# Token gather of the first feed-forward group moved behind the experts' matrix products, conversions given later steps, and the last output stored in four pieces

## The chip, the cores and the metric

The kernel runs on one core of one Trainium2 chip. The metric is the device time of one execution in microseconds (us). A core has five instruction streams, each in order: TensorE (PE in the rows; its weight loads are PEld), VectorE (DVE), ScalarE (ACT), GpSimd (POOL) and SyncE (SP), which issues most of the DMA transfers. A name with a q behind it (SPq, ACTq) is the sequencer of that stream, which decodes, branches and waits.

## The reference, cut to what matters

Three layers follow each other on 3072 tokens of width 384. Attention by a delta rule over 768 positions gives x; a router picks one of eight experts for each token; then a dense feed-forward layer runs over all tokens. The change lies where the second and the third layer meet, and at the end of the third.

```python
for e in range(E):                      # experts, E = 8, F = 1024
    mask = e_idx == e
    h = np.maximum(x[mask] @ w1[e], 0.0)
    out[mask] = gate_w[mask, None] * (h @ w2[e])
...
h = x @ w_in                            # feed-forward, d_ff = 2048
g = h * (1.0 / (1.0 + np.exp(-h)))
return (g @ w_out).astype(np.float32)
```

Every product is made in three passes over operands split into a high and a low part (high times high, high times low, low times high), so one tile of 128 inner rows costs three matmuls.

## The kernel before

**Experts.** `Experts.regular` (L1111) walks nine slots of tokens, five of 256 and four of 512, and each slot in eight chunks of 128 hidden units: 72 steps. A step splits the chunk's two weight tiles (`split`, L1016 on ACT, L1017 on DVE; the tiles are called wRH for w1 and wKT for w2), makes the hidden units (`first`, nine matmuls of 128x512 into ph, L1057, then L1060 on ACT and L1061 on DVE) and adds the chunk before it into the output banks (`second`, twelve matmuls of 128x384 into poe, L1068). When a slot is done, four copies (L1093, ACT) put its rows into the buffers ysb, and four indirect DMAs of POOL (L1095) scatter them to the tokens' places in the DRAM tensor ys. The first chunk of the last slot is followed by a branch for tokens that exceed the nine slots (`extra`, L1159); it is not taken here.

**Feed-forward.** `Ffn` walks six groups of 512 tokens. `tokens(g)` (L1275) gathers a group: SP loads 768 KB of ys into fy (L1278), PE transposes it by 3 times 4 matmuls with the identity into the banks fpt (L1282), and ACT (L1283) and DVE (L1284) split it into fxh and fxl. `group` (L1287) then makes sixteen chunks f: `first(f)` is nine matmuls of 128x512 into fph (L1298), a sigmoid (L1301, ACT), a product (L1303, DVE) and the split into fgh (L1305, ACT) and fgl (L1307, DVE); `second(f)` is twelve matmuls of 128x384 into four output banks fpo (L1315), one for each block of 128 tokens. At the end four copies, two on ACT and two on DVE (L1334), and one store of SP (L1335) bring the group out. The group at index g reads the block (g + 3) % 6 of ys, so the first group reads block 3. The last slot of the experts writes blocks 0 to 2 only, so the first group has to wait for the last slot but one.

**What sets the order.** Instructions are traced in program order and then placed by a scheduler, which moves them inside each engine as their inputs allow. Three numbers of `PLAN` (L35) bear on the change. `tok` is the step behind which the gather of the first group is traced (L1450); `n0` and `npre` spread 40 pieces of weight conversion for the feed-forward layer over the steps (L1446): behind step i, (i + 1 - n0) * npre / (72 - n0) pieces have been traced. These conversions are loads of SP (L1176) and elementwise work of DVE and ACT (L1187 to L1196). `tc.issue_after(x)` is a rule for the scheduler: what is traced inside its block comes behind x on x's engine. `experts.mark` is the last traced matmul of L1068.

Of the kernel before, what the change touches and what calls it, by code (L numbers as in the profile page):

```python
# [31 lines left out]
    hold=[17, 19, 21, 13],  # L32


    fin=10, fin1=19, fin2=30, fin3=36, n0=37, npre=40, tok=68,  # L35
)


# [1161 lines left out]
class Ffn:  # L1200
# [86 lines left out]
    def group(self, g, x, nxt, fill=()):  # L1287
        nc, P = self.nc, self.P
        xh, xl = x
        po = [P[p].tile([128, 384], F32, tag=p, name=f"fpo{g}_{c}") for c, p in enumerate(("pm", "pm", "pa", "pa"))]  # L1290

        def first(f):
            fs = slice(128 * f, 128 * f + 128)
            ph = P["pa"].tile([128, 512], F32, tag="pa", name=f"fph{g}_{f}")
            n = 0
            for k in range(3):
                for a, b in ((self.ih, xh), (self.ih, xl), (self.il, xh)):
                    nc.tensor.matmul(ph, a[:, k, fs], b[:, k, :], start=(n == 0), stop=(n == 8))  # L1298
                    n += 1
            sg = self.take("sg")  # L1300
            nc.scalar.activation(sg, ph, AF.Sigmoid)  # L1301
            gv = self.take("gv")
            nc.vector.tensor_tensor(gv, ph, sg, op=ALU.mult)  # L1303
            gh = self.take("gh")
            self.marks = [nc.scalar.copy(gh, gv).ins]  # L1305
            gl = self.take("gl")
            self.marks.append(nc.vector.tensor_tensor(gl, gv, gh, op=ALU.subtract).ins)  # L1307
            return gh, gl

        def second(f, gh, gl):  # L1310
            oh, ol = self.o[f]
            for c in range(4):
                cs = slice(128 * c, 128 * c + 128)
                for i, (a, b) in enumerate(((gh, oh), (gh, ol), (gl, oh))):
                    nc.tensor.matmul(  # L1315
                        po[c], a[:, cs], b, start=(f == 0 and i == 0), stop=(f == 15 and i == 2)
                    )

        prev = None
        for f in range(16):  # L1320
            cur = first(f)
            for fn in fill[f : f + 1]:
                with self.tc.issue_after(self.marks[0]), self.tc.issue_after(self.marks[1]):
                    fn()
            if f == 8 and nxt is not None:
                self.x = self.tokens(nxt)
            if prev is not None:
                second(f - 1, *prev)
            prev = cur
        second(15, *prev)  # L1330
        yield
        ob = P["fo"].tile([128, 4, 384], F32, tag="ob", name=f"ob{g}")
        for c in range(4):
            (nc.vector.tensor_copy if c % 2 else nc.scalar.copy)(ob[:, c, :], po[c])  # L1334
        nc.sync.dma_start(self.out.rearrange("(b t p) d -> t p b d", b=4, p=128)[g], ob)  # L1335

    def run(self, x, fill, spare):

# [8 lines left out]
def cut(t, sizes):  # L1347

    out, at = [], 0
    for n in sizes:  # L1350
        out.append(t[:, at : at + n])
        at += n
    return out
# [6 lines left out]
def expert_buffers(ar, ld, fw, f):  # L1360

    b = {}
    b["raw1"] = [rest(ar.tile([128, 3072], F32, tag="KQ0", name="raw1"), 1024)]
    kb = ar.tile([128, 4096], F32, tag="KB", name="raw2")
    b["raw2"], b["ysb"] = [rest(kb[:, 0:3072], 384)], cut(kb[:, 3072:3840], [384] * 2)
    hs = cut(ar.tile([128, 1024], F32R, tag="KQ1", name="hs"), [256] * 4)
    b["hh"], b["hl"] = hs[0:2], hs[2:4]
    ws = sum((cut(ar.tile([128, 1536], F32R, tag=t, name=f"w{t}"), [384] * 4) for t in ("RH", "KT")), [])
    for i, name in enumerate(("h1", "l1", "h2", "l2")):
        b[name] = [rest(x, 128) if i < 2 else x for x in ws[2 * i : 2 * i + 2]]  # L1370
    xs = [rest(ld.tile([128, 768], F32R, tag="kr", name=f"xhl{i}", bufs=4), 256) for i in range(4)]
    b["xh"], b["xl"] = xs[0:2], xs[2:4]

    o = fw.tile([128, 6144], F32R, tag="o1", name="pairs")
    b["xh2"] = [f.bufs["xh"][0], rest(o[:, 0:1536], 512)]
    b["xl2"] = [f.bufs["xl"][0], rest(o[:, 1536:3072], 512)]
    hs = cut(o[:, 3072:5120], [512] * 4)
    b["hh2"], b["hl2"] = hs[0:2], hs[2:4]
    b["xg"] = cut(ld.tile([128, 768], F32, tag="sq", name="xg", bufs=1), [384] * 2)
    b["xg2"] = b["xg"] + cut(f.P["f0"].tile([128, 768], F32, name="xg2"), [384] * 2)  # L1380
    return b


def ffn_buffers(ar):

    b = {x: [rest(ar.tile([128, 1536], F32R, tag=t, name=f"f{x}2"), 512)] for x, t in (("xh", "RH"), ("xl", "KT"))}
    kb = cut(ar.tile([128, 4096], F32, tag="KB", name="fy2"), [1536] + [512] * 4)
    b["y"], b["sg"], b["gv"] = [rest(kb[0], 384)], kb[1:3], kb[3:5]
    b["gh"] = cut(ar.tile([128, 1024], F32R, tag="KQ1", name="fgh"), [512] * 2)
    b["gl"] = cut(ar.tile([128, 1024], F32R, tag="KQ0", name="fgl"), [512] * 2)  # L1390
    return b


@with_exitstack
def fused_kernel(ctx: ExitStack, tc, q, k, v, beta, mod, w_gate, bias, w1, w2, w_in, w_out, out):
    nc = tc.nc

    def pool(stack, name, bufs=1, **kw):
        return stack.enter_context(tc.tile_pool(name=name, bufs=bufs, **kw))

    N, D = out.shape
    P = {
        "dram": pool(ctx, "dram", space=DRAM), "cc": pool(ctx, "cc"),
        "pa": pool(ctx, "pa", 5, space=PSUM), "pm": pool(ctx, "pm", 3, space=PSUM),
    }
    ident = P["cc"].tile([128, 128], F32, name="ident")
    make_identity(nc, ident)

    xs = P["dram"].tile([N, D], F32, name="xs")
    ys = P["dram"].tile([N, D], F32, name="ys")  # L1410
    P["rc"] = pool(ctx, "rc")

    with ExitStack() as moe:
        for name in ("ar", "ld"):
            P[name] = pool(moe, name, side="right")
        rank = ExitStack()
        P["rs"] = pool(rank, "rs", side="right")
        with ExitStack() as att:
            for name in ("ac", "ln"):
                P[name] = pool(att, name)  # L1420
            for name in ("sm", "y"):
                P[name] = pool(att, name, 2)
            attn = Attention(tc, ident, P, q, k, v, beta, xs)
            router = Router(tc, ident, P, attn.B, attn.T, w_gate, bias, mod)
            attn.run(router.load, router.logits, router.gate, router.wave)
        P["fw"], P["f0"] = pool(ctx, "fw"), pool(ctx, "f0")
        f = Ffn(tc, ident, P, w_in, w_out, ys, out)
        experts = Experts(tc, ident, P, router, w1, w2, xs, ys, expert_buffers(P["ar"], P["ld"], P["fw"], f))
        raw = ctx.enter_context(ExitStack())
        P["fr"] = pool(raw, "fr", 2)  # L1430
        n0, n1, at = PLAN["n0"], 9 * 8, 0
        fill = []
        P["rb"] = Views([P["fw"].tile([128, 6144], F32, tag=tag, name="scratch") for tag in ("il", "o0")])
        for i, _ in enumerate(experts.regular()):
            if i == PLAN["fin"]:
                steps = router.wave(attn.T - 1)
                next(steps)
            if i in (PLAN["fin1"], PLAN["fin2"], PLAN["fin3"]):
                with tc.issue_after(experts.mark):
                    next(steps, None)  # L1440
            if i == PLAN["fin3"]:
                rank.close()
                room = pool(raw, "fe").tile([128, 1536], F32, name="ysb2")
                experts.bufs["ysb2"] = cut(room, [384] * 4)
                fill = f.chain(f.inner() + f.outer(range(0, 8), "o0"))
            to = max(0, (i + 1 - n0) * PLAN["npre"] // (n1 - n0))  # L1446
            for fn in fill[at:to]:
                fn()
            at = max(at, to)
            if i == PLAN["tok"]:  # L1450
                x0 = f.tokens(0)
        fill += f.chain(f.outer(range(8, 16), "o1"))

        def spare():
            raw.close()
            return pool(ctx, "fo", 2)

        f.add(ffn_buffers(P["ar"]))
        f.run(x0, fill[at:], spare)
# [32 lines left out]
```

## Time and profile before

| What | us |
|---|---|
| Median of 3 runs | 1022.76 |
| Lowest and highest run | 1019.37, 1027.38 |
| The profiled execution, its own time | 1020.31 |
| The profiled execution, its span | 1018.6 |
| PE busy in the span | 912.6 |

The span goes from the first to the last instruction of the profiled execution; 1.7 us of its own time lie around it. All rows below are from that execution, and their times are counted from the span's start. The attention fills the span to about 370 us, the experts' steps run to about 608 us, and the six feed-forward groups end at 1018.6 us. A releaser that a row names is inferred from semaphore events, and ends of matmuls are modelled.

### The profile page before, as it was taken

To read this page: it belongs to the slowest core of one execution; us is meant where nothing else is said; L and a number is where in the kernel's file an instruction comes from. 1 tells how busy PE (TensorE), PEld (TensorE's weight loads), DVE (VectorE), ACT (ScalarE), POOL (GpSimd) and SP (SyncE) were. 2 spreads that over 40 slices of the span, in tenths; PEclk is the share of its full clock that TensorE was granted. 3 is DMA by queue.
4 is the path that set the end of the run, shared out by engine and by line. 5 is a ranking of instruction groups with operands and counts; after the bars stand their busy time and mean duration, and the time that the engine had idled before them with its cause. 6 is when DMAs were issued, how large, how long until landed. Compare 5 with 4: busy or idle time off the path is not lost. (4 is left out here: it accounts for less than half of the span.)

```text
span 1018.6 us, 22789 instructions
## 1 busy us (share of the span) xinstructions
PE 912.6 (90%) x8934; PEld 823.1 (81%) x8934; DVE 653.8 (64%) x1802; ACT 531.3 (52%) x1142; POOL 140.7 (14%) x129
## 2 busy tenths in 40 slices
PE   4427788888889999999999799999999999999997
PEld 4426777777778988888889699999998989999996
DVE  7999998989984459999994246643334333333332
ACT  6655978888756746655664354433233323332322
POOL 5462311010200011242330101000000000000000
PEclk9776999999989999999999899999999999999999
DMA  6864444341454152176664121101001000000000
GB/s 131 169 141 87 89 110 95 88 105 43 106 167 92 50 174 90 40 236 218 221 203 136 63 82 61 62 32 32 1 32 32 7 25 1 32 1 1 32 1 31
DMA packets 157668, 84.42 MB, mean 83 GB/s; under 512 B 125449, under 2 KB 150039, under 8 KB 157552
## 3 DMA queue, kind: packets, MB, share of 16 engines
q1 hardware_dynamic: 154224, 73.04, 27.2%
q0 software_dynamic: 3328, 9.83, 3.0%
q8 instruction: 72, 1.18, 0.5%
q14 instruction: 44, 0.36, 0.1%
HBM read 69.74 MB, written 20.84 MB: 89 GB/s over the span
## 5 line engine op out<-in xcount | busy, mean ns | idle before, releaser
L1315 PE MATMUL fpo<-o,fgh 128*128 128x384 f32 x768 | 184.3, 338 | 0.0
L1303 DVE TENSOR_TENSOR fy<-fph,fy 128x512 f32<-128x512 f32 x96 | 66.4, 692 | 160.6 <-ACT fy L1301 160.1
L1315 PEld LDWEIGHTS fpo<-o,fgh 128*128 128x128 f32 x768 | 139.2, 188 | 7.9 <-ACT fgh L1305 0.4
L1301 ACT ACTIVATE fy<-fph 128x512 f32<-128x512 f32 x96 | 57.4, 598 | 168.1 <-PE fph L1298 165.1
L1315 PE MATMUL fpo<-o,fgl 128*128 128x384 f32 x384 | 116.6, 338 | 0.0
L1307 DVE TENSOR_TENSOR fgl<-fy,fgh 128x512 fp32r<-128x512 f32 x96 | 66.4, 692 | 76.0 <-ACT fgh L1305 65.7
L1298 PE MATMUL fph<-fxh,ih 128*128 128x512 f32 x288 | 113.7, 395 | 0.0
L1298 PE MATMUL fph<-fxl,ih 128*128 128x512 f32 x288 | 113.3, 394 | 0.0
L1298 PE MATMUL fph<-fxh,il 128*128 128x512 f32 x288 | 113.1, 393 | 0.0
L1305 ACT CAST fgh<-fy 128x512 fp32r<-128x512 f32 x96 | 59.7, 622 | 82.7 <-DVE fy L1303 44.3
L316 DVE TENSOR_TENSOR A<-A,tmp 128x126 f32<-128x126 f32 (+20 forms) x336 | 85.0, 288 | 0.2
L230 PE MATMUL gr<-RHs,KTs 128*128 128x128 f32 x384 | 60.1, 305 | 27.3 <-ACT KTs L219 14.7
L230 PEld LDWEIGHTS gr<-RHs,KTs 128*128 128x128 f32 x384 | 52.4, 212 | 35.9 <-ACT KTs L219 20.3
L1068 PE MATMUL poe<-wKT,pairs 128*128 128x384 f32 x384 | 77.2, 347 | 3.1 <-ACTq L1159 3.1
L308 DVE TENSOR_TENSOR tmp<-A,L 128x126 f32<-128x126 f32 (+20 forms) x336 | 77.3, 267 | 0.3
L1068 PEld LDWEIGHTS poe<-wKT,pairs 128*128 128x128 f32 x384 | 69.3, 193 | 6.6 <-ACTq L1159 3.5
L1315 PEld LDWEIGHTS fpo<-o,fgl 128*128 128x128 f32 x384 | 71.1, 188 | 0.5
L1016 ACT CAST wRH<-raw 128x384 fp32r<-128x384 f32 x72 | 36.8, 514 | 49.8 <-PE ph L1057 44.2
L1298 PEld LDWEIGHTS fph<-fxl,ih 128*128 128x128 f32 x288 | 54.1, 188 | 10.5
L1298 PEld LDWEIGHTS fph<-fxh,il 128*128 128x128 f32 x288 | 54.1, 188 | 9.6
L1298 PEld LDWEIGHTS fph<-fxh,ih 128*128 128x128 f32 x288 | 54.1, 188 | 9.0
L1017 DVE TENSOR_TENSOR wKT<-raw,wKT 128x384 fp32r<-128x384 f32 x72 | 39.9, 554 | 31.2 <-ACT wKT L1016 30.9
(427 smaller groups left out, 1838.0 us busy)
## 6 DMA issues: line engine op xcount, KB each, us to landing
raw<-in_moe_w_dram SPq DMA_DIRECT2D x72, 384.0 KB
kn<-KQ SPq DMA_DIRECT2D x12, 512.0 KB
ri<-in_moe_w_in_dram SPq DMA_DIRECT2D x12, 512.0 KB
ro<-in_moe_w_out_dram SPq DMA_DIRECT2D x16, 384.0 KB
kr<-in_k_dram SPq DMA_DIRECT2D x48, 96.0 KB
KQ<-in_q_dram SPq DMA_DIRECT2D x48, 96.0 KB
KI<-kn SPq DMA_DIRECT2D x48, 96.0 KB
Z<-in_v_dram SPq DMA_DIRECT2D x24, 192.0 KB
```

The costliest lines, as they stand in the source:

```text
L230: nc.tensor.matmul(gr[:, j], self.KT[r][:, k, w, :], RH[:, k, :, w, :], start=True, stop=True)
L308: nc.vector.tensor_tensor(tv, r[:, :, j : j + 1].to_broadcast([128, c, n]), L[:, j : j + 1, j + 1 :].to_broadcast([128, c, n]), op=ALU.mult,)
L316: ins = nc.vector.tensor_tensor(r[:, :, j + 1 :], r[:, :, j + 1 :], tv, op=ALU.add)
L1016: nc.scalar.copy(hi, raw)
L1017: nc.vector.tensor_tensor(lo, raw, hi, op=ALU.subtract)
L1068: self.mark = nc.tensor.matmul(po[t], a[:, cs], b, start=(c == 0 and i == 0), stop=(c == F - 1 and i == 2)).ins
L1298: nc.tensor.matmul(ph, a[:, k, fs], b[:, k, :], start=(n == 0), stop=(n == 8))
L1301: nc.scalar.activation(sg, ph, AF.Sigmoid)
L1303: nc.vector.tensor_tensor(gv, ph, sg, op=ALU.mult)
L1305: self.marks = [nc.scalar.copy(gh, gv).ins]
L1307: self.marks.append(nc.vector.tensor_tensor(gl, gv, gh, op=ALU.subtract).ins)
L1315: nc.tensor.matmul(po[c], a[:, cs], b, start=(f == 0 and i == 0), stop=(f == 15 and i == 2))
```

## The change

Four things are edited. `tok` goes from 68 to 70, and the gather of the first group is traced inside `issue_after(experts.mark)`. `n0` goes from 37 to 40, so the 40 pieces of conversion are spread over 32 steps in place of 35. In the last group, the matmuls of `second(14)` and `second(15)` are traced block by block, both chunks for one block of tokens before the next block. And the last group's output is stored by four DMAs of 192 KB, each traced behind the copy of its block, in place of one of 768 KB. The other groups keep their order.

```diff
--- before.py
+++ after.py
@@ -32,7 +32,7 @@
     hold=[17, 19, 21, 13],
 
 
-    fin=10, fin1=19, fin2=30, fin3=36, n0=37, npre=40, tok=68,
+    fin=10, fin1=19, fin2=30, fin3=36, n0=40, npre=40, tok=70,
 )
 
 
@@ -1307,13 +1307,13 @@
             self.marks.append(nc.vector.tensor_tensor(gl, gv, gh, op=ALU.subtract).ins)
             return gh, gl
 
-        def second(f, gh, gl):
+        def second(f, gh, gl, cs=range(4)):
             oh, ol = self.o[f]
-            for c in range(4):
-                cs = slice(128 * c, 128 * c + 128)
+            for c in cs:
+                rows = slice(128 * c, 128 * c + 128)
                 for i, (a, b) in enumerate(((gh, oh), (gh, ol), (gl, oh))):
                     nc.tensor.matmul(
-                        po[c], a[:, cs], b, start=(f == 0 and i == 0), stop=(f == 15 and i == 2)
+                        po[c], a[:, rows], b, start=(f == 0 and i == 0), stop=(f == 15 and i == 2)
                     )
 
         prev = None
@@ -1324,15 +1324,25 @@
                     fn()
             if f == 8 and nxt is not None:
                 self.x = self.tokens(nxt)
-            if prev is not None:
+            if prev is not None and (f < 15 or nxt is not None):
                 second(f - 1, *prev)
-            prev = cur
-        second(15, *prev)
+            if f < 15 or nxt is not None:
+                prev = cur
+        if nxt is not None:
+            second(15, *prev)
+        else:
+            for c in range(4):
+                second(14, *prev, range(c, c + 1))
+                second(15, *cur, range(c, c + 1))
         yield
         ob = P["fo"].tile([128, 4, 384], F32, tag="ob", name=f"ob{g}")
+        ov = self.out.rearrange("(b t p) d -> t p b d", b=4, p=128)[g]
         for c in range(4):
             (nc.vector.tensor_copy if c % 2 else nc.scalar.copy)(ob[:, c, :], po[c])
-        nc.sync.dma_start(self.out.rearrange("(b t p) d -> t p b d", b=4, p=128)[g], ob)
+            if nxt is None:
+                nc.sync.dma_start(ov[:, c], ob[:, c, :])
+        if nxt is not None:
+            nc.sync.dma_start(ov, ob)
 
     def run(self, x, fill, spare):
 
@@ -1448,7 +1458,8 @@
                 fn()
             at = max(at, to)
             if i == PLAN["tok"]:
-                x0 = f.tokens(0)
+                with tc.issue_after(experts.mark):
+                    x0 = f.tokens(0)
         fill += f.chain(f.outer(range(8, 16), "o1"))
 
         def spare():
```

What the built programs show of it, at three places. On PE, at the last slot of the experts, these rows stand around the gather before (poe1_12 to poe1_15 are the output banks of the slot's four token blocks, ph1_12_3 to ph1_12_7 its hidden chunks 3 to 7, fpt0_0 the first transposed part of the first group):

```order
L1057 MATMUL ph1_12_4_12604<-pairs_5842,wRH_5836 128x512 x2
L1282 MATMUL fpt0_0_12638<-ident_66,fy_5830 128x128
L1068 MATMUL poe1_12_8264<-wKT_5837,pairs_5842 128x384 x2
L1068 MATMUL poe1_13_8265<-wKT_5837,pairs_5842 128x384 x2
L1068 MATMUL poe1_14_8266<-wKT_5837,pairs_5842 128x384
L1068 MATMUL poe1_12_8264<-wKT_5837,pairs_5842 128x384
L1068 MATMUL poe1_13_8265<-wKT_5837,pairs_5842 128x384
L1068 MATMUL poe1_14_8266<-wKT_5837,pairs_5842 128x384 x2
L1068 MATMUL poe1_15_8267<-wKT_5837,pairs_5842 128x384 x3
L1057 MATMUL ph1_12_4_12604<-pairs_5842,wRH_5836 128x512 x7
L1282 MATMUL fpt0_0_12638<-ident_66,fy_5830 128x128
L1068 MATMUL poe1_12_8264<-wKT_5837,pairs_5842 128x384
```

And now:

```order
L1068 MATMUL poe1_12_8264<-wKT_5837,pairs_5842 128x384
L1068 MATMUL poe1_13_8265<-wKT_5837,pairs_5842 128x384
L1068 MATMUL poe1_14_8266<-wKT_5837,pairs_5842 128x384
L1068 MATMUL poe1_15_8267<-wKT_5837,pairs_5842 128x384
L1282 MATMUL fpt0_0_12704<-ident_66,fy_5830 128x128 x4
L1282 MATMUL fpt0_1_12711<-ident_66,fy_5830 128x128 x4
L1282 MATMUL fpt0_2_12718<-ident_66,fy_5830 128x128 x4
L1068 MATMUL poe1_12_8264<-wKT_5837,pairs_5842 128x384 x2
L1068 MATMUL poe1_13_8265<-wKT_5837,pairs_5842 128x384 x2
L1057 MATMUL ph1_12_7_12727<-pairs_5842,wRH_5836 128x512 x9
L1068 MATMUL poe1_12_8264<-wKT_5837,pairs_5842 128x384
L1068 MATMUL poe1_13_8265<-wKT_5837,pairs_5842 128x384
```

The first transpose stood inside chunk 4, directly behind its second matmul, and the twelve were spread over the rest of chunk 4 and chunk 5. Now all twelve stand in one block, behind the last matmul of `second(5)`; 48 matmuls of poe and 25 of ph that stood behind the first transpose stand ahead of it. On ACT and DVE the three L1283 and three L1284 move with them, from between chunks 5 and 6 to between chunks 6 and 7.

On SP the end of the program reads before:

```order
L1278 DMA fy2_12789<-ys_72 128x4x384
L1335 DMA out_0_dram<-ob2_14231 128x4x384
L1335 DMA out_0_dram<-ob3_14679 128x4x384
L1335 DMA out_0_dram<-ob4_15127 128x4x384
L1335 DMA out_0_dram<-ob5_15553 128x4x384
L1487 UNCONDITIONAL_BRANCH
```

And now:

```order
L1345 DMA out_0_dram<-ob1_13783 128x4x384
L1278 DMA fy2_12789<-ys_72 128x4x384
L1345 DMA out_0_dram<-ob2_14231 128x4x384
L1345 DMA out_0_dram<-ob3_14679 128x4x384
L1345 DMA out_0_dram<-ob4_15127 128x4x384
L1343 DMA out_0_dram<-ob5_15553 128x384 x4
```

The last store has become four. On PE, though, the last rows stand as they stood before (fpo5_0 to fpo5_3 are the last group's four banks):

```order
L1315 MATMUL fpo5_0_15133<-o1_12786,fgl_12791 128x384
L1315 MATMUL fpo5_1_15134<-o1_12786,fgl_12791 128x384
L1315 MATMUL fpo5_2_15135<-o1_12786,fgl_12791 128x384
L1315 MATMUL fpo5_3_15136<-o1_12786,fgl_12791 128x384
L1315 MATMUL fpo5_0_15133<-o1_12786,fgh_12790 128x384 x2
L1315 MATMUL fpo5_1_15134<-o1_12786,fgh_12790 128x384 x2
L1315 MATMUL fpo5_2_15135<-o1_12786,fgh_12790 128x384 x2
L1315 MATMUL fpo5_3_15136<-o1_12786,fgh_12790 128x384 x2
L1315 MATMUL fpo5_0_15133<-o1_12786,fgl_12791 128x384
L1315 MATMUL fpo5_1_15134<-o1_12786,fgl_12791 128x384
L1315 MATMUL fpo5_2_15135<-o1_12786,fgl_12791 128x384
L1315 MATMUL fpo5_3_15136<-o1_12786,fgl_12791 128x384
```

The blocks still run side by side: the scheduler kept chunk 14 for all four banks ahead of chunk 15, and the high passes ahead of the low ones.

On SP the loads of the converted weights read, before (-) and now (+):

```order
-L1176 DMA ri_1_7319<-in_moe_w_in_dram 128x1024
-L1176 DMA ri_2_7361<-in_moe_w_in_dram 128x1024
-L1003 ISA
-L1003 DMA raw_5834<-in_moe_w_dram 128x2x384
-L1000 ISA
-L1000 DMA raw_5833<-in_moe_w_dram 128x3x256
+L1176 DMA ri_1_7377<-in_moe_w_in_dram 128x1024
+L1176 DMA ri_2_7471<-in_moe_w_in_dram 128x1024
+L1003 ISA
+L1003 DMA raw_5834<-in_moe_w_dram 128x2x384
+L1000 ISA
+L1000 DMA raw_5833<-in_moe_w_dram 128x3x256
```

Only buffer numbers differ. The same holds for every load of L1176 and for every conversion on DVE and ACT up to the gather: the scheduler placed them where they stood. Of SP's three loads of fy that stand together there, the one for the second group now stands ahead of the one for the third.

## Rows read from the trace of the kernel before

**Rows 1.** The page, part 1: busy us, share of the span, instructions

```profile
PE 912.6 (90%) x8934; PEld 823.1 (81%) x8934; DVE 653.8 (64%) x1802; ACT 531.3 (52%) x1142; POOL 140.7 (14%) x129
```

**Rows 2.** Waits of PE from 555 to 612 us: total, times, longest

```profile
PE fpt L1282 <- DMA fy<-ys: 3.7, 1, 3.7
PE poe L1068 <- ACTq L1159: 3.1, 1, 3.1
```

**Rows 3.** The chain that ended last, 563 to 603 us: start, us, what

```profile
571.07 4.34 DMA ys<-ysb,sidx
...
575.48 4.70 DMA fy<-ys
...
580.55 3.08 PE poe L1068 x12
...
588.15 0.98 PE fpt L1282 x9
...
590.36 2.10 PE ph L1057 x9
...
597.71 2.09 PE poe L1068 x12
```

**Rows 4.** Stretches: us, busy of PE, PEld, DVE, ACT, POOL, PEclk, DMA, GB/s

```profile
576.50:580.20 3.70, 0.01 (x1) 0.00 (x0) 0.85 (x2) 0.09 (x1) 0.00 (x0) 1.00 0.75 213
581.24:584.72 3.48, 3.48 (x13) 3.19 (x12) 0.51 (x1) 0.51 (x1) 0.00 (x0) 0.52 0.00 0
564.30:567.70 3.40, 3.40 (x12) 3.20 (x11) 1.50 (x3) 0.94 (x3) 0.98 (x1) 0.50 0.15 58
567.80:576.50 8.70, 8.70 (x41) 7.14 (x40) 3.75 (x7) 3.89 (x8) 1.90 (x2) 1.00 0.11 42
600.00:640.00 40.00, 40.00 (x210) 36.56 (x209) 24.79 (x48) 20.55 (x36) 4.35 (x4) 1.00 0.22 71
```

**Rows 5.** Instructions that use the tile fpt: duration ns min/median/max

```profile
L1283 ACT CAST fxh<-fpt x18: 578/586/608, 588.6 to 914.1; 128x512 fp32r<-128x512 f32 x18
L1284 DVE TENSOR_TENSOR fxl<-fpt,fxh x18: 680/682/693, 589.2 to 914.7; 128x512 fp32r<-128x512 f32 x18
```

**Rows 6.** Instructions in order of time, 600 to 612 us

```profile
607.50 0.61 ACT L1189 ACTIVATE ro8e<-ro8e,shift 128x384 int32<-128x384 int32 x1
...
609.91 0.54 ACT L1195 CAST o<-ro8f 128x384 fp32r<-128x384 f32 x1
```

**Rows 7.** Instructions in order of time, 996 to 1019 us

```profile
1008.51 0.60 ACT L1301 ACTIVATE fy<-fph 128x512 f32<-128x512 f32 x1 [2.23 <-PE fph L1298]
...
1010.52 0.69 DVE L1307 TENSOR_TENSOR fgl<-fy,fgh 128x512 fp32r<-128x512 f32 x1 [0.69 <-ACT fgh L1305]
...
1012.03 0.86 PE L1315 MATMUL fpo<-o,fgl 128*128 128x384 f32 x4
1012.40 0.86 ACT L1334 COPY ob<-fpo 128x384 f32<-128x384 f32 x2 [1.92 <-PE fpo L1315]
1012.57 1.02 DVE L1334 COPY ob<-fpo 128x384 f32<-128x384 f32 x2 [1.36 <-PE fpo L1315]
1013.67 0.37 SPq L1335 DMA_DIRECT2D out_dram<-ob  x1
```

**Rows 8.** Stretches of the last store, columns as in rows 4

```profile
1012.90:1014.40 1.50, 0.00 (x0) 0.00 (x0) 0.70 (x2) 0.36 (x1) 0.00 (x0) 1.00 0.00 0
1014.40:1016.80 2.40, 0.00 (x0) 0.00 (x0) 0.00 (x0) 0.00 (x0) 0.00 (x0) 0.59 0.89 328
```

**Rows 9.** Waits of SP from 1000 to 1019 us

```profile
SPq L1487 <- DMA out_dram<-ob: 2.9, 1, 2.9
```

**Rows 10.** A store of 192 KB, xs, that starts alone: its issue on SP

```profile
366.61 0.34 SPq L449 DMA_DIRECT2D xs<-Y  x1
```

**Rows 11.** Stretches behind that issue, columns as in rows 4

```profile
367.40:367.60 0.20, 0.20 (x3) 0.20 (x2) 0.00 (x0) 0.00 (x0) 0.00 (x0) 1.00 0.63 230
...
367.80:368.00 0.20, 0.20 (x4) 0.20 (x3) 0.00 (x0) 0.00 (x0) 0.00 (x0) 1.00 0.89 323
```

## The prediction

> **What bounds the kernel now.** The page's first part says which engine to follow: PE is busy for 912.6 of 1018.6 us and DVE, the next, for 653.8 [rows 1]. So a change pays only where PE stands still or runs slowly, or behind PE's last matmul. The second view is the list of waits around the place of the change, the end of the experts' steps. PE waits twice there: 3.7 us for the load of fy, at the first transpose of the first group, and 3.1 us for ACT's branch [rows 2]. The change touches the first only. The chain of waits says why fy is late: the last scatter of the slot before starts at 571.07 and lands 4.34 us later, SP then issues the load of fy at 575.48, and that takes 4.70 us to land, at 580.18 [rows 3]. PE reached the transpose at 576.5.
>
> The third view, stretches with the granted clock, shows a second price. In the gap PE has no matmul to run; from 581.24 to 584.72 it then works at about half the clock, 0.52 of full speed, that is at 1.2 instead of 2.4 GHz [rows 4]. The gap at the branch has such a tail too, 0.50 from 564.30 to 567.70. Between the two, from 567.8 to 576.5, PE is busy for 8.70 of 8.70 us at full clock, and from 600 to 640 us, in the first group, for 40 of 40. The view in order of time, last, shows the end: four copies, one issue, one transfer of 768 KB.
>
> **The gather, part by part.** Ahead of the first transpose stand now 48 more matmuls of poe and 25 more of ph. At full clock 12 of poe take 2.09 us and 9 of ph 2.10 [rows 3], so 48 x 0.174 = 8.4 and 25 x 0.233 = 5.8, in all 14.2 us. PE comes to the transposes at 576.5 + 14.2 = 590.7. The load of fy waits for the same scatter as before, and nothing that SP or POOL does ahead of it has moved, so it lands at 580.2 still: 10.5 us early. The wait of 3.7 us goes whole.
>
> Is something else late in those 14.2 us? The matmuls need their split weights and hidden units from ACT and DVE. These stand in the same order as before on both, but for the three casts and subtractions of the gather, which are now a chunk later. I followed the chunks by hand with the durations of the rows and found each input ready before PE reaches it; and 567.8 to 576.5 is the same mixture of work, with ACT busy for 3.89 and DVE for 3.75 of 8.70 us and no gap on PE [rows 4]. Behind the transposes the first group's first matmul comes after 12 of poe and 9 of ph, 4.2 us. The block of twelve transposes takes 12 x 0.109 = 1.3 us (nine took 0.98 [rows 3]), as much as they took apart. Even if all three casts (0.59 each) and the last subtraction (0.68) came behind the last transpose, the operands would be there after 2.4 us [rows 5]. So nothing takes the wait's place here: minus 3.7 us.
>
> The clock: 3.48 us at half the clock are 1.74 us of lost work. The matmuls say the same from their side: the 12 of poe from 580.55 took 3.08 us where 12 take 2.09, 1.0 us more, and the rest lies in the matmuls that follow [rows 3]. With no gap I expect no slow stretch behind it. Bounds: 0, if the clock falls there anyway, and 1.74. I take 1.7, because the stretch ahead of the gap, which has matmuls without a break, holds full clock up to the gap itself [rows 4].
>
> The other order of SP's loads of fy costs nothing: the second group's transposes come behind chunk 8 of the first group, more than 30 us after either place.
>
> **The conversions.** Nothing: the built program has every one of these loads and conversions where it was, though the trace positions differ. The scheduler had already put them where their buffers and loads let them be. The same holds for the block-by-block tracing of the last two chunks: PE's last rows are unchanged, so no bank is done earlier than before. Of this pair of edits only the four stores are left.
>
> **The last store.** Before, the last copy ends at 1012.57 + 1.02 = 1013.59, SP issues at 1013.67, data move from about 1014.5 to 1016.7, with the engines nearly full the whole time [rows 7, 8], and SP waits 2.9 us from the end of its issue, 1014.04, to 1016.94 [rows 9]. Now the first store needs ACT's first copy only. ACT's two copies take 0.86 us together from 1012.40, so the first ends near 1012.9, and SP can issue at 1012.96, 0.71 us earlier. The four issues take about 0.35 each: 0.34 for a store of 192 KB of the same shape [rows 10], 0.37 for the large one. They start at 1012.96, 1013.31, 1013.67 and 1014.03; each copy is done by then. That small store's data appear some 0.86 us behind its issue (0.63 of a stretch of 0.2 us that begins at 367.40) and move in about 0.55 us [rows 11]. So the pieces' data follow each other without a hole, from 1013.8 on for the same 2.1 to 2.2 us, and end 0.7 us earlier. That is one bound. The other: the pieces do not overlap at all, and each pays its way in, 0.86, its data, 0.55, and its way out, 0.2 (data end 1016.74, SP goes on at 1016.94). Then 4 x 1.6 = 6.4 us from 1012.96 end at 1019.4, 2.4 later than before. I take minus 0.7: the rows nearest to it are those of the large store, whose many rows of 1536 bytes go out without a hole, and the pieces consist of the same rows.
>
> A rule speaks against this part. The Trainium skill, "DMA: Bandwidth & Descriptors", gives about 2.0 us fixed for each DMA plus the bytes at 436 GB/s (section "Anatomy of one DMA", fitted to DMAs issued by GpSimd), and in "Rules for kernel authors" it asks to coalesce. By it the one store would take 3.8 us (the trace has 3.27 from issue to SP's going on), and four in series 9.8 us, 5.3 us worse in the end, which would eat the gain of the gather and leave about 1020.2; if the fixed parts overlap, it costs nothing. No run here shows which.
>
> **The sum.** 1020.31 - 3.7 - 1.7 - 0.7 = 1014.2 us, from the profiled execution's own time. That execution lies 2.45 us below the median of the three runs; from the median the same 6.1 us give 1016.7. The runs before spread over 8 us, and neither start is better, so I take the middle, 1015.4 (1.2 above the sums below).
>
> **The rivals.**
> - Only the gap goes, the slow stretch stays, because the branch's gap some 13 us earlier is what the clock answers to. For it: that gap has a slow tail as well. Against it: full clock from 567.8 to 576.5. 1020.31 - 3.7 - 0.7 = 1015.9, and with the 1.2 1017.1.
> - The pieces of the store are served one after another, the upper bound above: 1020.31 - 5.4 + 2.4 = 1017.3, so 1018.5.
> - The wait is replaced: PE now arrives at the first group 5.4 us earlier, and ACT has the four copies of L1093 and a conversion of w_out ahead of the sigmoid of chunk 1, where it had the sigmoid first. If PE stands as long there as it stood at fy, and the clock falls again, only the store is left: 1019.6, so 1020.8. Against it: in my hand-made schedule the second chunk's fgl is ready some 3.7 us before PE comes to it.
> - Slower: the conversions in the first group. ACT's cast for w_out (L1195) now stands ahead of the cast of fgh in the first two pieces. From the sigmoid to the end of fgl takes 1008.51 to 1011.21, 2.7 us [rows 7], and PE gives it one chunk, 12 matmuls of poe's kind and 9 of ph's, 4.2 us. A piece's work on ACT, 0.61 + 0.54 [rows 6], between the links makes it 3.85, still covered. If it took over 1.5 us for each piece, PE would stand at each. With the whole 1.15 us bare for all eight pieces: 8 x 1.15 = 9.2, 1020.31 - 6.1 + 9.2 = 1023.4, so 1024.6. Against it: 600 to 640 holds half of these pieces with PE busy for 40 of 40 us [rows 4].
>
> **How the numbers follow.** The forecast has 0.62, the clock that falls anyway 0.14, the stores in series 0.08, the replaced wait 0.12, the slower case 0.04. The range of 1010.5 to 1021.5 takes in the two starts of the sum, the bounds of the clock and of the store, and the replaced wait; it leaves out the slower case and the outer part of the runs' spread. One per cent is about what a measurement of this kernel can tell from no change. Faster by that means below 1012.5, counted from the median; the forecast lies 2.9 us above it, and with runs 8 us apart some three in ten of its chance fall below: 0.19, and 0.01 from the others. Slower by as much needs 1033, which only the slower case or a bad set of runs would reach: 0.04. The rest, 0.76, is within one per cent.
>
> **What would show it.** Right: no wait of PE for fy; full clock from 568 us to the end; second(7) of the last slot done about 5.4 us earlier; PE without gaps in the first group; four issues of SP about 0.35 us apart, the first some 0.7 us ahead of the last copy's end, and data without holes. Wrong: a PE wait of over 1 us between 576 and 612 us, a clock of 0.5 anywhere there, a store whose data come in four separate bursts, or conversions that stand elsewhere in time than before by more than the gain.

## The result

The changed kernel is faster by 0.9 per cent in these runs, and by 0.65 in a second measurement.

| | kernel before | changed kernel |
|---|---|---|
| time, median (lowest to highest), us | 1024.63 (1019.37 to 1027.38), 4 runs | 1013.74 (1012.48 to 1017.10), 4 runs |
| ratio, 95% interval | | 0.9908 [0.9879, 0.9937] |
| profiled execution: time, span, us | 1020.31, 1018.6 | 1013.98, 1012.3 |
| PE's last matmul to the end of the span, us | 1012.89 to 1018.6: 5.7 | 1007.55 to 1012.3: 4.75 |

The prediction was 1015.4 us with a range of 1010.5 to 1021.5. A second measurement of the same change (below) gave 0.9935 [0.9909, 0.9961]. Both intervals hold 0.9928, which is what 1015.4 is of 1022.76, the median of the three runs before. Ratios leave out runs in the chip's slower state: one run, of the twelve with xs below.

The page of the changed kernel, part 1, answers to [rows 1]: PE is busy for 3.2 us less in a span that is 6.3 us shorter, still 90% of it.

```profile
PE 909.4 (90%) x8934; PEld 821.1 (81%) x8934; DVE 655.8 (65%) x1802; ACT 531.4 (52%) x1142; POOL 144.2 (14%) x129
```

The waits of PE from 555 to 615 us in the changed kernel answer to [rows 2]. The line of fpt on fy is gone; the branch stays.

```profile
PE poe L1068 <- ACTq L1159: 3.1, 1, 3.1
```

The chain that ended last, 560 to 604 us, changed kernel (start, us, what), answers to [rows 3]. It holds no DMA any more, only PE: the twelve transposes in one piece, the twelve matmuls of poe that close the last slot, and the first of fpo at 602.49. The old chain had these same first four of fpo at 607.86, so 5.4 us have gone by then.

```profile
588.74 2.09 PE poe L1068 x12
590.83 1.31 PE fpt L1282 x12
...
599.71 2.09 PE poe L1068 x12
601.80 0.69 PE fph L1298 x3
602.49 0.71 PE fpo L1315 x4
```

SP in order of time, 572 to 583 us, changed kernel: the issue of the load of fy.

```profile
575.75 0.38 SPq L1278 DMA_DIRECT2D fy<-ys  x1
```

Stretches of the changed kernel, columns as in [rows 4]: behind the branch, from there to the transposes, in the first group, and two around the landing of fy.

```profile
564.60:568.00 3.40, 3.40 (x12) 3.22 (x12) 1.52 (x3) 0.84 (x3) 1.01 (x2) 0.52 0.15 58
568.10:590.80 22.70, 22.70 (x116) 20.38 (x115) 9.34 (x16) 8.14 (x16) 1.84 (x2) 1.00 0.17 52
600.00:640.00 40.00, 40.00 (x210) 36.60 (x209) 27.30 (x53) 20.00 (x36) 4.35 (x4) 1.00 0.26 81
...
577.00:580.40 3.40, 3.40 (x19) 3.10 (x18) 1.09 (x3) 0.71 (x2) 0.00 (x0) 1.00 0.65 224
580.40:581.20 0.80, 0.80 (x6) 0.76 (x6) 0.45 (x1) 0.80 (x2) 0.00 (x0) 1.00 0.00 0
```

The load moves as late as before (issue 575.48 then, 575.75 now) and the DMA engines fall silent at 580.4; PE is busy through it and comes to the transposes 10.3 us later, at 590.7. The half-clock stretch behind the branch is there as it was, at 0.52; the second one is not: 1.00 from 568.1 to 590.8, and on through the first group.

The end in order of time, changed kernel, answers to [rows 7]:

```profile
1006.69 0.86 PE L1315 MATMUL fpo<-o,fgl 128*128 128x384 f32 x4
1007.06 0.86 ACT L1341 COPY ob<-fpo 128x384 f32<-128x384 f32 x2 [1.92 <-PE fpo L1315]
1007.24 1.02 DVE L1341 COPY ob<-fpo 128x384 f32<-128x384 f32 x2 [1.36 <-PE fpo L1315]
1007.57 1.81 SPq L1343 DMA_DIRECT2D out_dram<-ob  x4
```

The four stores by their line (duration of one issue min/median/max in ns, first and last start), changed kernel:

```profile
L1343 SPq DMA_DIRECT2D out_dram<-ob x4: 344/393/405, 1007.6 to 1009.0; - x4
```

Their stretches, changed kernel, answer to [rows 8]:

```profile
1008.00:1008.50 0.50, 0.00 (x0) 0.00 (x0) 0.26 (x1) 0.00 (x0) 0.00 (x0) 1.00 0.14 52
1008.50:1009.00 0.50, 0.00 (x0) 0.00 (x0) 0.00 (x0) 0.00 (x0) 0.00 (x0) 1.00 0.98 356
1009.00:1009.50 0.50, 0.00 (x0) 0.00 (x0) 0.00 (x0) 0.00 (x0) 0.00 (x0) 1.00 1.04 378
...
1010.00:1010.50 0.50, 0.00 (x0) 0.00 (x0) 0.00 (x0) 0.00 (x0) 0.00 (x0) 1.00 0.96 372
1010.50:1011.00 0.50, 0.00 (x0) 0.00 (x0) 0.00 (x0) 0.00 (x0) 0.00 (x0) 1.00 0.16 55
```

The first store goes out while DVE still copies (it is busy for 0.26 us of the first stretch), and the data of the four pieces run together at 356 to 378 GB/s.

### The profile page after: what moved, and what is told of

It reads as the page before. It is cut to its first block, busy times and chain, and to the rows that moved or that the text cites. A ratio compares the mean times of both kernels' runs of the same rounds, so it can differ in the third digit from the quotient of the medians.

```text
span 1012.3 us, 22794 instructions
## 1 busy us (share of the span) xinstructions
PE 909.4 (90%) x8934; PEld 821.1 (81%) x8934; DVE 655.8 (65%) x1802; ACT 531.4 (52%) x1142; POOL 144.2 (14%) x129
## 5 line engine op out<-in xcount | busy, mean ns | idle before, releaser
L1057 PE MATMUL ph<-xhl,wRH 128*128 128x256 f32 x360 | 54.5, 291 | 4.8 <-DVE wRH L1017 4.2
```

Source lines behind the costliest of these rows:

```text
L1057: nc.tensor.matmul(ph, a[:, k, :], b[:, k, :], start=(i == 0), stop=(i == 8))
```

## The experiments

Eight kernels ran, in two sets of four; each set shares its runs of the kernel before (23 in the first, median 1024.30; 22 in the second, median 1026.82). My theory: the gain is PE's wait for fy with the half-clock work behind it, plus about 0.7 us of the store. The rivals: the place of the twelve transposes or the conversions matter by themselves; the store's pieces add up in series.

**One part of the change at a time.** First the gather alone (the store and n0 as before):

```
-    n0=37, npre=40, tok=68,
+    n0=37, npre=40, tok=70,
...
             if i == PLAN["tok"]:
-                x0 = f.tokens(0)
+                with tc.issue_after(experts.mark):
+                    x0 = f.tokens(0)
```

> Only the gather of the first group is moved (step 70, behind the experts' matmuls); one store, conversions as before. Theory A (the prediction's sum): the wait for fy and the slow stretch go, 5.4 us less than before, a ratio of 0.9947, and the store's 0.7 us are missing against the whole change. Theory B (the wait for fy is longer in most runs than in the profiled one, and the move takes it whole in each): 8 to 10 us less, near 0.991. Profile in both: no wait of PE for fy, full clock from 568 us to the end of PE's work.

Measured: 1016.77 us (6 runs), 0.9924 [0.9894, 0.9953]. Most of the gain is here. The interval holds the 0.9947 of theory A and the 0.991 of theory B, so these runs do not decide between the two sizes. Stretches of this kernel, from PE's first matmul behind the branch to the transposes:

```profile
566.57:572.57 6.00, 6.00 (x17) 5.61 (x18) 1.86 (x4) 1.85 (x4) 1.97 (x2) 0.50 0.10 35
572.60:594.50 21.90, 21.90 (x110) 19.64 (x110) 8.95 (x16) 7.63 (x15) 1.34 (x2) 1.00 0.16 53
```

No wait for fy and no slow stretch behind it. But the slow stretch behind the branch is 6 us long in this execution, where the changed kernel had 3.4 in the same instructions.

The new end alone (the functions of the diff's second part in the kernel before):

```
-        second(15, *prev)
...
+            for c in range(4):
+                second(14, *prev, range(c, c + 1))
+                second(15, *cur, range(c, c + 1))
...
+            if nxt is None:
+                nc.sync.dma_start(ov[:, c], ob[:, c, :])
```

> Only the last group is edited: block-by-block tracing and four stores; the gather stands where it stood. Theory A: PE's wait for fy and the slow stretch stay (about 3.7 and 3.5 us), and the tail from PE's last matmul to the span's end is 0.7 us shorter than the 5.7 us of before. Rival (stores served one after another): the tail is 2.4 us longer. By the timed runs 0 to 1 us less than before. Theory B expects the same of the time, and a wait for fy in this profile that differs from 3.7 us by some us.

Measured: 1022.66 us (12 runs), 0.9977 [0.9959, 0.9995]. A small gain that the runs just resolve. PE's last four matmuls and the issue of the stores, in order of time:

```profile
1016.67 0.86 PE L1315 MATMUL fpo<-o,fgl 128*128 128x384 f32 x4
...
1017.55 1.80 SPq L1343 DMA_DIRECT2D out_dram<-ob  x4
```

From PE's end at 1017.53 to the end of the span (1022.2) it takes 4.67 us instead of 5.7: 1.0 less, where theory A had 0.7. The wait for fy is in its place; PE's line in the list of waits, and the stretches of the gap and of the work behind it, in this kernel:

```profile
PE fpt L1282 <- DMA fy<-ys: 4.1, 1, 4.1
```

```profile
582.40:584.30 1.90, 0.00 (x0) 0.00 (x0) 0.00 (x0) 0.00 (x0) 0.00 (x0) 0.50 0.77 290
584.30:588.50 4.20, 4.16 (x14) 4.16 (x15) 0.00 (x0) 0.00 (x0) 0.00 (x0) 0.50 0.00 0
```

The clock is at half already inside the gap, and stays there for over 4 us of work: both the wait and the slow stretch are longer than in the execution from which I had taken their prices.

The later due time of the conversions alone:

```
-    n0=37, npre=40, tok=68,
+    n0=40, npre=40, tok=68,
```

> Only n0 goes from 37 to 40. The built program has the instructions of before in the same order on all five engines. Theory A: the same time as before, ratio 1.000 within its interval; so this pair also shows how far two runs of one program differ. A rival by which the spread itself gains (buffers in another rotation, other addresses): 3 us or more less. Theory B: the same time as before, and its profile shows another length of the wait for fy.

Measured: 1024.28 us (12 runs), 1.0007 [0.9985, 1.0029]: no change that the runs resolve, as the unchanged order of its instructions said. So its profile is a second look at the kernel before, and this one shows a wait nearly twice as long. PE's line in the list of waits, then the stretches in the gap and behind it, then POOL's first two scatters of the slot before, all of this kernel:

```profile
PE fpt L1282 <- DMA fy<-ys: 6.7, 1, 6.7
```

```profile
578.30:580.60 2.30, 0.00 (x0) 0.00 (x0) 0.00 (x0) 0.00 (x0) 0.00 (x0) 0.53 0.81 303
580.60:585.10 4.50, 4.47 (x14) 4.45 (x15) 0.00 (x0) 0.11 (x1) 0.00 (x0) 0.50 0.00 0
```

```profile
560.01 0.98 POOL L1095 DMA_INDIRECT ys<-ysb,sidx  x1 [15.89 <-ACT ysb L1093]
565.13 0.99 POOL L1095 DMA_INDIRECT ys<-ysb,sidx  x1 [4.13 <-ACT wRH L1016]
```

The longer wait has two sources. The second scatter started 5.12 us after the first, where the kernel before has 3.43 (560.98 to 564.41). Counted from PE's first matmul behind the branch, fy came 1.4 us later (17.9 in place of 16.5 us). And PE had no slow stretch behind the branch here, so by the same count it came to the transpose 1.6 us sooner, only to wait there. Together these are the 3.0 us between 3.7 and 6.7.

The whole change once more, with the same runs of before:

> The whole change once more, beside its parts on the same chip. Theory A: 6.1 us less than before, ratio 0.994. Theory B: 9 to 11 us less, 0.990 to 0.991. It should equal the sum of the three parts to within 2 us.

Measured: 1017.82 us (6 runs), 0.9935 [0.9909, 0.9961], nearer to the 0.994 of theory A. The parts taken one by one multiply to 0.9924 x 0.9977 x 1.0007 = 0.991. By the medians the whole gains 6.5 us and the parts together 9.2: they miss the expected 2 us, but by less than the intervals leave open.

**The wait removed without moving anything on PE.** The kernel before, with the first group's tokens loaded from xs in place of ys, so that the load need not wait for the experts' scatters (this leaves the experts out of the first group's result; SP issues the load at 370.05 us):

```
-        nc.sync.dma_start(y, self.ys.rearrange("(t b p) d -> t p b d", b=4, p=128)[(g + 3) % 6])
+        src = self.ys if g else self.xs
+        nc.sync.dma_start(y, src.rearrange("(t b p) d -> t p b d", b=4, p=128)[(g + 3) % 6])
...
```

> The kernel before, but the first group's load reads the attention's output xs in place of ys, so it waits for no scatter (this leaves the experts out of the first group's result). The order on PE, DVE, ACT and POOL is that of before, transposes inside chunk 4 and all; on SP the load stands far earlier. Theory A (the price is the wait and the slow clock behind it): PE never waits at fpt, no clock of 0.5 between 573 and 590 us unless it belongs to the branch's gap, and the time is that of e1, 6 to 9 us under before, ratio 0.991 to 0.994. Rival (the place counts: twelve transposes in one block, and fewer breaks between matmuls, gain by themselves): no more than half of that.

Measured: 1019.61 us (12 runs), 0.9933 [0.9908, 0.9958]. The transposes stand where they stood before the change, spread over chunks 4 and 5, and the gain of the gather is there. A stretch of this kernel that holds all of them (the first starts at 578.47, the last nine at 584.61):

```profile
572.00:600.00 28.00, 28.00 (x147) 25.18 (x146) 11.76 (x20) 11.16 (x21) 1.74 (x2) 1.00 0.17 52
```

No wait, no slow stretch. So neither the block of twelve nor its place is needed for the gain; that fy is there in time is.

**The transposes two chunks earlier.** The gather issued behind the experts' mark, but at position 68:

```
             if i == PLAN["tok"]:
-                x0 = f.tokens(0)
+                with tc.issue_after(experts.mark):
+                    x0 = f.tokens(0)
```

> Step 68 as before, but the gather is pinned behind the experts' matmuls: the twelve transposes stand in one block behind second(3), 24 matmuls of poe and 7 of ph behind their old place, about 5.8 us later, in place of 14.2. Theory A: PE reaches them about 24 us behind its branch; the load of fy landed 21.8 to 23.8 us behind the branch in the profiles so far, so the wait is 0 to 1 us, no slow stretch follows, and the time is within 2 us of e1 (ratio 0.991 to 0.995). Rival (only the full distance covers it): a wait of 3 us or more and the time of before.

Measured: 1019.95 us (10 runs), 0.9941 [0.9914, 0.9967]. The twelve transposes stand as one block here too, but behind `second(3)`: 24 matmuls of poe and seven of ph later than in the kernel before. PE's line in the list of waits of this kernel, and its stretches on both sides of that wait:

```profile
PE fpt L1282 <- DMA fy<-ys: 1.4, 1, 1.4
```

```profile
568.96:585.90 16.94, 16.94 (x84) 15.08 (x84) 7.83 (x14) 6.85 (x14) 2.95 (x3) 1.00 0.19 59
587.41:600.00 12.59, 12.59 (x67) 11.29 (x68) 4.35 (x8) 4.20 (x8) 0.00 (x0) 1.00 0.21 64
```

This place is just short of enough: the wait is 1.4 us, where theory A had 0 to 1. This wait has no slow stretch behind it. The branch, with a gap of 3.06 us, has none in this execution either, so it stays open whether a short gap spares the clock as such.

**The store in eight pieces of 96 KB.** This asks whether the pieces' costs overlap, by making more of them:

```
-                nc.sync.dma_start(ov[:, c], ob[:, c, :])
+                for h in range(2):
+                    nc.sync.dma_start(ov[:, c, 192 * h : 192 * h + 192], ob[:, c, 192 * h : 192 * h + 192])
```

> The whole change with the last output stored in eight pieces of 96 KB (two for each copy). Theory A (pieces overlap; the end is set by the last issue): eight issues of about 0.45 us from the first to the last take 3.2 us in place of 1.4, so the data have holes and end about 1.5 us later than with four, and the tail from PE's last matmul to the end is 4.8 + 1.5 = 6.3 us. Rival (each piece pays its way in series): over 10 us.

Measured: 1018.93 us (one run, no interval). From PE's last matmul, which ends at 1011.13, to the end of the span at 1017.2 it takes 6.07 us, against 4.75 with four pieces and 5.7 with one. The end in order of time of this kernel, its issues by line, and two of the stretches in which its data move:

```profile
1010.27 0.86 PE L1315 MATMUL fpo<-o,fgl 128*128 128x384 f32 x4
...
1011.15 3.76 SPq L1344 DMA_DIRECT2D out_dram<-ob  x8
```

```profile
L1344 SPq DMA_DIRECT2D out_dram<-ob x8: 345/408/445, 1011.1 to 1014.5; - x8
```

```profile
1012.00:1013.00 1.00, 0.00 (x0) 0.00 (x0) 0.00 (x0) 0.00 (x0) 0.00 (x0) 1.00 0.61 201
1013.00:1014.00 1.00, 0.00 (x0) 0.00 (x0) 0.00 (x0) 0.00 (x0) 0.00 (x0) 1.00 0.61 201
```

Now the issue sets the pace: one store each 0.48 us (3.4 us for seven steps), 98,304 bytes in that time is 205 GB/s, and the stretches show 201 at a DMA share of 0.61. With four pieces the same step carries twice the bytes, 418 GB/s by the 0.47 us between their issues, which is more than the 356 to 378 that the transfer moves: there the data set the pace. In series, with the prediction's 0.86 in and 0.2 out for each and half of its 0.55 for the data, eight pieces would have taken 8 x 1.335 = 10.7 us.

**The end really by row blocks.** The last twelve matmuls are pinned, so that the banks are done one after the other, as the change's code reads but the built program does not do:

```
-            for c in range(4):
-                second(14, *prev, range(c, c + 1))
-                second(15, *cur, range(c, c + 1))
+            second(14, *prev)
+            (gh, gl), (oh, ol), pin = cur, self.o[15], self.tail
+            for c, i in ((0, 0), (0, 1), (1, 0), (1, 1), (0, 2), (1, 2), (2, 0), (2, 1), (2, 2), (3, 0), (3, 1), (3, 2)):
...
+                with self.tc.issue_after(pin):
+                    pin = nc.tensor.matmul(
```

> The whole change, and the last twelve matmuls pinned in the order that its text asks for: blocks 0 and 1 end first, then 2, then 3. Theory A (the scheduler undid the block order, and the copies and stores wait for PE's last four matmuls): the copies start about 0.9 us earlier against PE's last matmul, the first store goes out ahead of PE's end, and the tail behind PE's last matmul shrinks from 4.8 us to about 3.8, PE's end at the same place or up to 0.3 later. By the timed runs 0 to 1 us under the whole change. Rival (the tail is the last store's own way, whatever goes ahead): the tail stays at 4.8 us.

Measured: 1019.01 us (7 runs), 0.9909 [0.9878, 0.9940]. The end in order of time of this kernel:

```profile
1013.86 0.56 DVE L1346 COPY ob<-fpo 128x384 f32<-128x384 f32 x1 [0.70 <-PE fpo L1339]
...
1014.20 1.82 SPq L1348 DMA_DIRECT2D out_dram<-ob  x4
...
1014.53 0.34 PE L1339 MATMUL fpo<-o,fgl 128*128 128x384 f32 x1
1014.91 0.56 DVE L1346 COPY ob<-fpo 128x384 f32<-128x384 f32 x1 [0.49 <-PE fpo L1339]
```

The first store now starts 0.67 us ahead of PE's last end (1014.87), and from there to the end of the span (1018.9) it takes 4.03 us instead of 4.75. That 0.7 us is seen in the profile alone; the timed runs cannot tell 0.9909 from the change's own ratios. By the profile it is the best version that ran.

## Why the prediction was right, step by step

The times of single executions spread over 8 us, but the profiles can be compared far more closely once three things are taken out of each: what comes before the branch, PE's wait for fy, and what the slow clock costs. The table does that. "From" is the start of PE's first matmul behind the branch, "length" the span's end less that. A cost of the clock is the sum of (1 less PEclk) over stretches of 1 us behind the branch or behind the wait. "Left" is the length less the three columns before it.

| kernel | from | length | wait for fy | clock, branch | clock, fy | left |
|---|---|---|---|---|---|---|
| before | 563.75 | 454.85 | 3.71 | 1.70 | 1.71 | 447.7 |
| conversions alone | 562.74 | 456.76 | 6.70 | 0 | 2.33 | 447.7 |
| gather alone | 566.57 | 450.53 | 0 | 3.04 | 0 | 447.5 |
| from xs | 565.88 | 449.32 | 0 | 1.70 | 0 | 447.6 |
| gather two chunks earlier | 568.96 | 449.54 | 1.45 | 0 | 0 | 448.1 |
| store alone | 567.44 | 454.76 | 4.14 | 1.71 | 2.30 | 446.6 |
| changed kernel | 563.94 | 448.36 | 0 | 1.70 | 0 | 446.7 |
| the whole again | 564.62 | 448.38 | 0 | 1.71 | 0 | 446.7 |
| eight pieces | 567.52 | 449.68 | 0 | 1.71 | 0 | 448.0 |
| blocks in order | 569.94 | 448.96 | 0 | 3.11 | 0 | 445.9 |

What is left has one value for each kind of end: 447.5 to 447.7 with one store (448.1 in one profile, a difference I can't place), 446.6 to 446.7 with four, 448.0 with eight, 445.9 with the blocks in order. So nothing but the wait, the clock and the store moved, and each term can be judged.

- **The wait, minus 3.7.** Right in mechanism: it went whole, PE reached the transposes at 590.7 as forecast, and nothing took its place; wait and clock together are the 5.4 us by which fpo comes earlier. The kernel with xs shows that the wait is the cause and not the order on PE. The size is taken up below.
- **The clock, minus 1.7.** Right in mechanism: in all six profiles without a wait for fy no slow stretch follows there, with the branch's own slow stretch still in place. That settles the first rival, the clock that falls anyway.
- **Both sizes were taken from the cheapest of three executions.** The wait and its clock cost 5.4 us in the execution that I read, 6.4 in the store's and 9.0 in the conversions' profile, 7.0 in the mean; the runs of the gather alone give 0.76% of 1024.3, 7.8 us, interval 4.8 to 10.9. By these profiles this is the term of the sum that was mis-sized; the runs by themselves do not exclude 5.4. An estimate from the other kernels whose load waits for the scatters says the same: SP's issue of fy plus 4.5 us for the load (4.39 to 4.70 where PE waited for it), less the time at which PE would have come to the old place ("from", 11.05 us of work and the branch's clock cost), gives waits of 3.5 to 7.4 us in nine profiles, 4.9 in the mean, where I had 3.7. The cause is in the two sources above. POOL's second scatter starts 3.40 to 5.78 us behind the first in the ten profiles, and the 3.43 of the profile that I read is the second shortest: when POOL's second scatter starts late, fy is late, and where PE runs fast behind the branch, it only waits longer.
- **The conversions, 0.** Right: 1.0007.
- **The block-by-block tracing, 0.** Right: PE's last rows are the same, and only pinning them gave something.
- **The store, minus 0.7.** Right in sign and kind, 0.95 by the two tails (5.7 and 4.75) and 1.0 by the table. The first issue stands 0.02 us behind PE's last end instead of 0.78, 0.76 earlier where I had 0.71. The issues are 0.47 apart, not 0.35, which costs nothing, because the data are slower still: they end near 1010.6, 3.0 behind PE's end, where they ended at 1016.74, 3.85 behind it. The remaining 0.1 lies behind the data and I have not traced it. By runs the store is worth 0.23%, interval 0.05 to 0.41.
- **The stores in series**, the second rival, would have cost 2.4 us. The data without holes, and the eight pieces, refute it. The Trainium skill, "DMA: Bandwidth & Descriptors" ("Anatomy of one DMA"), gives each DMA a fixed cost of about 2.0 us, by a fit to DMAs issued by GpSimd. By that figure four stores in series are 9.8 us, an estimate; the whole tail took 4.75, so these four stores did not pay it one after another.
- **The replaced wait and the conversions in the first group**, the third and fourth rivals: PE is busy for 40.00 of 40 us from 600 to 640 at full clock, and PE's list of waits is empty from 600 to 1012.
- **The start of the sum.** I took the middle between the profiled execution and the median of three runs, 1021.5. Later runs of the kernel before had medians of 1024.3 and 1026.8: the start was 3 to 5 us low. The gain by medians was 10.9 us the first time and 6.5 the second, where I had 6.1. A start that is too low and a gain that is too small partly make up for each other in the predicted time; that it came within 1.7 us of the measured 1013.74 is in part luck. Had I sized the gain by the mean of the three executions, 7.0 + 0.95 = 8.0 us or 0.78%, it would have stood inside both intervals; 6.1 us, 0.9940 by the median of before, stands inside the second only.

## What to carry to other kernels

The wait that ended on a DMA behind a chain of scatters was 3.7, 4.1 and 6.7 us long in three executions with the same order around it, because it is the difference of two paths. Before pricing the removal of such a wait from one profile, read the second path too, and say that whatever makes the waiting engine faster ahead of it only lengthens the wait. When executions spread more than the effect, take the stretch ahead of the change, the waits and the granted clock out of each profile; here that left 0.2 us between profiles of kernels with one store, one of them excepted, whose lengths differ by up to 7.4. Splitting the last store by the order in which its parts are ready paid here with 192 KB for each issue, 418 GB/s by the issues' step, and no longer with 96 KB, 205 GB/s: before splitting, compare that with what the transfer moves (356 to 378 GB/s). And code that was written block by block gave no earlier block until the built order was pinned.

## What was not expected of the hardware

The same untaken branch, with a gap of 3.1 to 3.5 us on PE, was followed in ten profiles by half-clock work that cost 0 us (two profiles), 1.70 or 1.71 (six), or 3.04 and 3.11 (two): three distinct sizes and nothing between. In the gather-alone profile PE's first matmul after the gap already ran at 0.50; in the store-alone profile the first microsecond was at 1.00 and the next at 0.51. The instructions were the same ahead of it, so a slow stretch read from one profile is one draw among several.

The other spread lies ahead of the branch. PE's first matmul behind it starts between 562.74 and 569.94 us in these profiles, and nothing of the edits lies before it but the load of xs in one kernel. Where in the attention and router stages these 7 us arise was not looked into.
